# Attention's pieces on SyncE's row: two rates for keys and queries, and the weight fetch ahead of the pieces

## The chip, the cores and the metric

The kernel runs on one core of a Trainium2 chip. The core has a matrix engine (TensorE, PE in the rows, with its weight loads shown apart as PEld), a vector engine (VectorE, DVE), a scalar engine (ScalarE, ACT), GpSimd (POOL) and SyncE (SP), which here issues the transfers between the chip's main memory (DRAM) and the core's own memory (SBUF). Every engine works its instructions off in one fixed row and stands still where the next of them waits for another engine or for a transfer. TensorE writes its products into PSUM, a small memory of eight banks.

The metric is the time of one execution on the device, in microseconds (us); the median of several runs counts.

## What is computed

Windowed attention with a few memory keys, then two products with a maximum between, then two products with a piecewise function between. All of it is float32.

```python
# attention: B, H, S, D = 4, 8, 768, 64; 8 memory keys
for c in range(24):                                   # chunks of 32 queries
    q_c   = q[:, :, 32*c : 32*c + 32]
    k_ctx = k[:, :, max(0, 32*c - 16) : min(S, 32*c + 32 + 8)]     # v_ctx alike
    s = concat([mem_k, k_ctx]) . q_c / 8
    out[:, :, 32*c : 32*c + 32] = softmax(s) @ concat([mem_v, v_ctx])
x = out as (3072 tokens, 512)
# first MLP, 512 -> 768 -> 512
h = max(x @ w1, x @ w2, x @ w3);  x = h @ w_out
# second MLP, 512 -> 2048 -> 512
h = x @ w_in
g = h where h >= 1, 0 where h <= -1, (h + 1)**2 / 4 between
out = g @ w_out2
```

## The kernel before

A float32 product is made of three faster ones: each operand is split into a high and a low part, and `mm3` (L499 to L501) adds high x high, high x low and low x high into the same bank. These three lines are most of TensorE's work.

The tokens go through the first MLP in six blocks of 512. Attention goes in 24 units of 128 tokens, four to a block. The loop over `order` (its body begins where `last_block = done = 0` is set) is one slot for each product group of the first MLP: a slot runs its products (`slot_l1` or `slot_l2`), then one `att_step()`, which is a sixth of an attention unit, then copies of finished products out of PSUM, splits, and last a few transfers. `steps(u)` yields the six parts of a unit: the first has the product with the values of the unit before (`st_o`, L426) and the scores (`st_s`, L378); the second asks for the next values (`load_v`, eight transfers at L265, always into the same buffer `vw`); the third flips keys and queries. So `part`, which is `done % 6`, counts slots within a unit, shifted by one: it is taken after `done` was raised.

**Keys and queries.** They come as many small transfers, called pieces here, because the transposes that "flip" them on VectorE want them laid out in a certain way: 32 rows of 32 elements for each chunk. `load_ks` puts 20 pieces for three units of keys into the list `queue` (16 of 32x12x32 elements and 4 narrow ones for the edge), ahead of whatever queries are still in it; they go into the buffer `kq`. `load_qs` appends 16 pieces for two units of queries (32x8x32 elements), which go in turn into two tiles `qs` and into `kT2`. `feed` takes pieces from the front of the list and issues them on SP, in each slot as many as a table says. `flip_k` and `flip_q` first issue whatever the list still holds (L352, L360), and then transpose what has come (L355, L356, L363).

**Weights of the second MLP.** Beside this, the loop prepares combined weights for the second MLP. `round_step` does one step of that for each slot, by the part: "p" (part 1) and "b" (part 5) combine on VectorE, "out a" (part 3) stores the weights combined last to DRAM (five stores, L948 to L952, for the first weights; two, L954 and L955, for the later ones) and has ScalarE take the absolute value of the next ones (`abs_w`, L134), and "in in" (part 4) fetches two more weights (`fetch_w`, L119 or L121) into a staging tile `st`, of which there are two. The fetch of part 4 writes the tile that the stores of part 3 have just read.

**SP's row.** Every transfer of the kernel is issued by SP, in the order in which the program is written (`manual_schedule`): pieces, values, stores, fetches, and outputs of finished blocks (`yd`, L1107). A transfer that must wait, for a buffer or for another transfer, holds all that stand behind it.

The lines of a slot around the change, and the table of parts:

```python
    BY_PART = "", "p", "", "out a", "in in", "b"
    ...
                part = 5 if s == 3 else done % 6
                feed((5, 6, 4, 6, 5, 1)[part])
                round_step(BY_PART[part].split() + (["a"] if s == 1 else []))
```

Of the kernel before, what the change touches and what calls it, by code (L numbers as in the profile page):

```python
# [64 lines left out]
def attention_then_two_mlps(ctx, tc, q, k, v, mem_k, mem_v, w1, w2, w3, w_mid, w_in, w_out, out):  # L65
# [218 lines left out]
    def fill_mk(u):  # L284
        b = u // UPB
        if held["kw"] != b:
            copy("km", u)(
                out=kw[:, :, :, 0:NM],
                in_=memkT[:, :, b:b + 1, :].to_broadcast([P, HP, NC, NM]))
            held["kw"] = b  # L290
# [18 lines left out]
    NB3 = 3 * NC  # L309
    ks = kq[:, 0:HP * (NB3 + 1) * CH].rearrange("p (h c d) -> p h c d", h=HP, d=CH)  # L310
    qs = {}
    queue = []

    def quadrants(src, h, t0, rows, n):
        for e in range(2):
            for x in range(2):
                yield (2 * e + x) * 32, src[2 * h + e, t0:t0 + n * CH, 32 * x:32 * x + 32].rearrange(
                    "(c t) d -> t c d", t=rows)

    def load_ks(g):  # L320
        b, s0 = divmod(3 * g, UPB)
        t0 = s0 * P - LEFT
        c0 = 1 if t0 < 0 else 0
        later = queue[:]
        del queue[:]
        for h in range(HP):
            for r, a in quadrants(k[b], h, t0 + c0 * CH, CH, NB3):
                queue.append(partial(nc.sync.dma_start, out=ks[r:r + CH, h, c0:c0 + NB3, :], in_=a))
        r0, c, t = (LEFT, 0, 0) if c0 else (0, NB3, S - LEFT)
        for e in range(2):  # L330
            for x in range(2):
                r = (2 * e + x) * 32 + r0
                queue.append(partial(
                    nc.sync.dma_start, out=ks[r:r + LEFT, :, c, :],
                    in_=k[b].rearrange("(h e) t d -> e t h d", e=2)[e, t:t + LEFT, :, 32 * x:32 * x + 32]))
        queue.extend(later)
# [11 lines left out]
                queue.append(partial(nc.sync.dma_start, out=qs[g][h // 2][r:r + CH, h % 2], in_=a))  # L348

    def flip_k(u):  # L350
        while queue:
            queue.pop(0)()  # L352
        c = u % 3 * NC
        fill_mk(u)
        nc.vector.transpose(out=kw[:, :, :, NM:NM + CH], in_=ks[:, :, c:c + NC, :])  # L355
        nc.vector.transpose(out=kw[:, :, :, NM + CH:NM + 2 * CH], in_=ks[:, :, c + 1:c + 1 + NC, :])  # L356

    def flip_q(u):
        while queue:
            queue.pop(0)()  # L360
        c = u % 2 * NC
        for i, t in enumerate(qs[u // 2]):
            nc.vector.transpose(out=qTb[u % 2][:, 2 * i:2 * i + 2], in_=t[:, :, c:c + NC, :])  # L363
# [129 lines left out]
    def att_step():  # L493
        for s in todo.pop() if todo else ():
            run(*s)
# [40 lines left out]
    def l1_split(j, f, m):  # L536
        if m == 2:
            split(("A", j, f), cur.pop(("t", j, f)), f"a{j}_{f}")
# [81 lines left out]
    def split_c():  # L620
        s = put[0]
        if s >= limit[0]:
            return
        n, k = divmod(s, 7)
        t = raw[2 * n + (k >= PARTS)][:, PRODUCTS[k][0] % PARTS]
        cs[s] = next_half()
        c = cs[s].rearrange("p (u f) -> p u f", u=2)
        nc.scalar.copy(out=c[:, 0], in_=t)  # L628
        nc.gpsimd.tensor_tensor(out=c[:, 1], in0=t, in1=c[:, 0].bitcast(F32), op=ALU.subtract)  # L629
        put[0] += 1  # L630
        if k in (PARTS - 1, 6) and loaded[0] < total // 7 * 2:
            del raw[2 * n + (k >= PARTS)]
            load_c(loaded[0])
            loaded[0] += 1
# [300 lines left out]

    fetched, rounded, kept = [2 * Q1 + 4], [Q1], []

    def feed(room):
        while queue and room > 0:
            queue.pop(0)()  # L940
            room -= 1

    def round_step(acts):
        if "out" in acts and kept:
            q, c, d = kept.pop(0)
# [28 lines left out]
    BY_PART = "", "p", "", "out a", "in in", "b"  # L974

    with tc.manual_schedule(engines={ENG.PE, ENG.DVE, ENG.Activation, ENG.Pool, ENG.SP}):
# [67 lines left out]
        def w_tile(name):  # L1044
            return wpool.tile([P, 2, TB], F32, tag="w", name=name)

        last_block = done = 0
        for s, (f, *a) in enumerate(order):
            j = a[0]
            if f is not slot_l2 and j == NB - 1 and last_block == 0:  # L1050
                while todo:
                    att_step()
                att.close()
                rp = ctx.enter_context(tc.tile_pool(name="rp", bufs=1, side="right"))
                last_block = s
                hb.append(rp.tile([P, TB], F32R, tag="hb0", name="hb0"))
                hb.extend(mx.tile([P, TB], F32R, tag="y", name=f"hb{i}", bufs=2) for i in (1, 2))
                fb.extend(rp.tile([P, TB], F32, tag=f"f{i}", name=f"f{i}") for i in range(6))
                hq["h12", 2] = [rp.tile([P, TB], F32, tag=f"h{i}", name=f"h12_{i}") for i in (4, 5)]
                for g in (0, 1):  # L1060
                    hq["h22", g] = rp.tile([P, 2, TB], F32, tag=f"a{g}", name=f"h22_{g}")
            made, out_now = unsplit[:], stores[:]
            del stores[:]
            f(*a)
            if last_block:
                made = unsplit[:]
            else:

                for _ in range(2 if s in (2, 3) else 1):
                    att_step()  # L1070
                    done += 1
                for _ in range(2):
                    if evictions:
                        evictions.pop(0)()

            for x in made:
                l1_split(*x)
                unsplit.remove(x)
            if last_block:
                t = s - last_block  # L1080
                round_step(["out"])
                if t == 1:
                    for g in (2, 3):
                        hq["h22", g] = w_tile(f"h22_{g}")
                for name in LAST_BLOCK.get(t, "").split():
                    if name == "c":
                        split_c()
                    elif name == "raw":
                        load_c(loaded[0])
                        loaded[0] += 1  # L1090
                    elif name == "r":
                        load_d(t - 4)
                    elif name == "d":
                        i = len(resident)
                        split_d(i)
                        if i + 2 < len(RESIDENT):
                            load_d(i + 2)
                    elif name == "E":
                        hq["h21", 0] = w_tile("h21_0")
                    else:  # L1100
                        prep(0, name)
            else:
                part = 5 if s == 3 else done % 6
                feed((5, 6, 4, 6, 5, 1)[part])
                round_step(BY_PART[part].split() + (["a"] if s == 1 else []))
                for store in out_now:
                    store()  # L1107
        for x in unsplit:
# [81 lines left out]
```

## Time and profile before

| | |
|---|---|
| median of 3 runs | 969.0 us (968.9 to 969.28) |
| the profiled execution | 968.48 us, of which its instructions span 966.7 us |
| mean granted clock of TensorE | 0.987 of full speed |
| TensorE busy | 945.5 us, 98% of the span |
| VectorE, ScalarE, GpSimd busy | 705.2, 542.2, 339.5 us |
| transfers | 142.81 MB, 148 GB/s on average, queue of the kernel's own transfers 51.2% of 16 DMA engines' time |

The loop with attention in it runs to about 440 us of the span; after it come the last block of the first MLP and the second MLP, which hold none of the pieces. In the rows below, a start is in us from the start of the span. "x8" is a number of instructions that are shown as one row, with the time from the first's start to the last's end. "SPq" is SP's row of issues: the time there is that of issuing, not of moving the data. "[3.32 <-ACT t L532]" is idle time ahead of an instruction and what ended it.

### The profile page before, as it was taken

The numbers are of one execution on the slowest core, as the hardware profiler recorded it, in microseconds if no ns is written. First come the engines' busy times: TensorE is split into PE (matmuls) and PEld (weight loads), VectorE is DVE, ScalarE is ACT, GpSimd is POOL, SyncE is SP. The second block draws the span as 40 slices with busy tenths as digits, with TensorE's granted clock in tenths as the row PEclk, the third lists the DMA queues.
The fourth block names the chain that finished last, engine by engine and source line by source line (L and its number), as shares of the span: only waits on it lengthen the run. The fifth ranks groups of instructions, "written<-read, shape, count | busy, mean of one in ns | idle before, by whom it ended". The sixth has DMA issues, their size and how long they took to land.

```text
span 966.7 us, 18906 instructions
## 1 busy us (share of the span) xinstructions
PE 945.5 (98%) x7090; PEld 777.7 (80%) x7090; DVE 705.2 (73%) x1001; ACT 542.2 (56%) x972; POOL 339.5 (35%) x330
## 2 busy tenths in 40 slices
PE   6799999999989999999999999999999999999998
PEld 5688887888868888888888888888888888888886
DVE  3999947687766777762436777997777998777855
ACT  5766644342324223322438777676777776777763
POOL 0000003222321010110656555555566555665542
PEclk8799999999999999999999999999999999999999
DMA  7886646657667576524314237525235644322723
GB/s 183 221 221 194 167 132 162 162 148 219 186 194 193 141 183 205 190 93 155 115 38 154 81 94 277 159 61 120 76 98 181 229 120 89 98 87 87 262 66 66
DMA packets 242779, 142.81 MB, mean 148 GB/s; under 512 B 174464, under 2 KB 210176, under 8 KB 242688
## 3 DMA queue, kind: packets, MB, share of 16 engines
q1 hardware_dynamic: 242688, 141.60, 51.2%
q8 instruction: 56, 0.92, 0.4%
q14 instruction: 35, 0.29, 0.1%
HBM read 109.71 MB, written 31.46 MB: 146 GB/s over the span
## 4 chain that ended last, share of the span: by engine, by line
PE 93%; DVE 2%; DMA 2%; SPq 1%; ACT 1%; issue 1%; POOL 0%; POOLq 0%; DVEq 0%; ACTq 0%
PE psums L499 29%; PE psums L501 28%; PE psums L500 28%; PE psums L426 2%; PE psums L378 2%; PE psums L410 1%; PE psums L273 1%; DMA kq<-in_k_dram 1%; DMA kq<-in_q_dram 0%; PE psums L304 0%; PE psums L1011 0%; DMA vw<-in_v_dram 0%; SPq L360 0%; SPq L265 0%; SPq L940 0%
## 5 line engine op out<-in xcount | busy, mean ns | idle before, releaser
L518 POOL TENSOR_TENSOR hl_a<-t,hh_a 128x512 fp32r<-128x512 f32 x30 | 41.0, 1366 | 394.3 <-ACT hh_a L516 375.8
L499 PE MATMUL psums<-xh,hi 128*128 128x512 f32 x432 | 173.4, 401 | 3.3 <-ACT t L532 3.3
L501 PE MATMUL psums<-xh,lo 128*128 128x512 f32 x432 | 169.4, 392 | 0.0
L500 PE MATMUL psums<-xl,hi 128*128 128x512 f32 x432 | 169.2, 392 | 0.2 <-DVE xl L440 0.2
L809 POOL TENSOR_TENSOR hb<-h,hb 128x512 fp32r<-128x512 f32 x72 | 99.5, 1382 | 92.5 <-PE psums L501 59.5
L801 ACT CAST hb<-h 128x512 fp32r<-128x512 f32 x144 | 88.8, 622 | 48.1 <-PE psums L500 46.5
L499 PEld LDWEIGHTS psums<-xh,hi 128*128 128x128 f32 x432 | 81.8, 189 | 20.3 <-ACT t L532 3.7
L501 PEld LDWEIGHTS psums<-xh,lo 128*128 128x128 f32 x432 | 81.7, 189 | 17.8
L534 DVE TENSOR_TENSOR t<-psums,t 128x512 f32<-128x512 f32 x72 | 49.4, 686 | 63.9 <-PE psums L501 63.9
L629 POOL TENSOR_TENSOR hb<-ra,hb 128x256 fp32r<-128x256 f32 x96 | 75.4, 797 | 58.7 <-ACT hb L628 56.3
L500 PEld LDWEIGHTS psums<-xl,hi 128*128 128x128 f32 x432 | 81.8, 189 | 16.5 <-DVE xl L440 0.7
L693 ACT ACTIVATE psums<-h 128x512 f32<-128x512 f32 x96 | 57.9, 603 | 59.9 <-DVE h L779 24.2
L501 PE MATMUL psums<-t,hb 128*128 128x512 f32 x192 | 74.8, 390 | 0.0
L500 PE MATMUL psums<-t,hb 128*128 128x512 f32 x192 | 74.7, 389 | 0.0
L499 PE MATMUL psums<-t,hb 128*128 128x512 f32 x192 | 74.7, 389 | 0.0
L629 POOL TENSOR_TENSOR hb<-rb,hb 128x256 fp32r<-128x256 f32 x72 | 55.7, 780 | 39.2 <-ACT hb L628 39.2
L807 DVE TENSOR_TENSOR hb<-psums,hb 128x512 fp32r<-128x512 f32 x66 | 44.9, 680 | 24.8 <-PE psums L501 21.3
L694 ACT ACTIVATE psums<-psums 128x512 f32<-128x512 f32 x96 | 55.9, 582 | 3.1
L499 PE MATMUL psums<-hh_a,hi 128*128 128x512 f32 x144 | 57.5, 399 | 0.0
L832 DVE TENSOR_TENSOR h<-h,h 128x1024 f32<-128x1024 f32 (+1 forms) x42 | 56.5, 1368 | 0.0
L500 PE MATMUL psums<-hl_a,hi 128*128 128x512 f32 x144 | 56.2, 390 | 0.0
L501 PE MATMUL psums<-hh_a,lo 128*128 128x512 f32 x144 | 56.2, 390 | 0.0
(145 smaller groups left out, 2244.9 us busy)
## 6 DMA issues: line engine op xcount, KB each, us to landing
t<-td SPq DMA_DIRECT2D x15, 1024.0 KB
ra<-cd SPq DMA_DIRECT2D x24, 512.0 KB
st<-in_moe_w_out_dram SPq DMA_DIRECT2D x22, 512.0 KB
st<-in_moe_w_dram SPq DMA_DIRECT2D x18, 512.0 KB
vw<-in_v_dram SPq DMA_DIRECT2D x152, 56.0 KB
st<-in_moe_w_in_dram SPq DMA_DIRECT2D x16, 512.0 KB
h<-yd SPq DMA_DIRECT2D x12, 512.0 KB
rb<-cd SPq DMA_DIRECT2D x24, 256.0 KB
```

What stands on the lines that cost most here:

```text
L499: nc.tensor.matmul(out, whi, xhi, start=first, stop=False)
L500: nc.tensor.matmul(out, whi, xlo, start=False, stop=False)
L501: nc.tensor.matmul(out, wlo, xhi, start=False, stop=last)
L518: e.tensor_tensor(out=lo, in0=h, in1=hi.bitcast(F32), op=ALU.subtract)
L534: nc.vector.tensor_tensor(out=cur["t", j, f], in0=s, in1=cur["t", j, f], op=ALU.max)
L629: nc.gpsimd.tensor_tensor(out=c[:, 1], in0=t, in1=c[:, 0].bitcast(F32), op=ALU.subtract)
L693: nc.scalar.activation(out=a, in_=x, func=AF.Relu, bias=0.5, scale=0.5)
L694: nc.scalar.activation(out=a, in_=a, func=AF.Square)
L801: nc.scalar.copy(out=hi, in_=x)
L807: nc.vector.tensor_tensor(out=lo, in0=y, in1=hi.bitcast(F32), op=ALU.subtract)
L809: nc.gpsimd.tensor_tensor(out=lo, in0=x, in1=hi.bitcast(F32), op=ALU.subtract)
L832: nc.vector.tensor_tensor(out=x, in0=y, in1=z, op=op)
```

## The change

No transfer and no instruction is added or taken away; the places of transfers on SP's row are changed.

- `send(n)` takes the place of `feed(room)` and of the loops in `flip_k` and `flip_q`. It also counts down `urgent`, the number of key pieces that are still in the list (they stand at its front).
- While there are key pieces in the list, the table is the old one: 5, 6, 4, 6, 5, 1 pieces for the six parts. While there are only queries, it is 3, 4, 2, 4, 3, 0. The table is chosen by what is in the list before a slot's pieces are sent.
- In part 4 `round_step`, with its fetch of two weights, comes ahead of the slot's pieces. In the other parts it stays behind them.

```diff
--- before.py
+++ after.py
@@ -309,13 +309,18 @@
     NB3 = 3 * NC
     ks = kq[:, 0:HP * (NB3 + 1) * CH].rearrange("p (h c d) -> p h c d", h=HP, d=CH)
     qs = {}
-    queue = []
+    queue, urgent = [], [0]
 
     def quadrants(src, h, t0, rows, n):
         for e in range(2):
             for x in range(2):
                 yield (2 * e + x) * 32, src[2 * h + e, t0:t0 + n * CH, 32 * x:32 * x + 32].rearrange(
                     "(c t) d -> t c d", t=rows)
+
+    def send(n):
+        for _ in range(min(n, len(queue))):
+            queue.pop(0)()
+            urgent[0] = max(urgent[0] - 1, 0)
 
     def load_ks(g):
         b, s0 = divmod(3 * g, UPB)
@@ -325,11 +330,13 @@
         del queue[:]
         for h in range(HP):
             for r, a in quadrants(k[b], h, t0 + c0 * CH, CH, NB3):
+                urgent[0] += 1
                 queue.append(partial(nc.sync.dma_start, out=ks[r:r + CH, h, c0:c0 + NB3, :], in_=a))
         r0, c, t = (LEFT, 0, 0) if c0 else (0, NB3, S - LEFT)
         for e in range(2):
             for x in range(2):
                 r = (2 * e + x) * 32 + r0
+                urgent[0] += 1
                 queue.append(partial(
                     nc.sync.dma_start, out=ks[r:r + LEFT, :, c, :],
                     in_=k[b].rearrange("(h e) t d -> e t h d", e=2)[e, t:t + LEFT, :, 32 * x:32 * x + 32]))
@@ -348,16 +355,14 @@
                 queue.append(partial(nc.sync.dma_start, out=qs[g][h // 2][r:r + CH, h % 2], in_=a))
 
     def flip_k(u):
-        while queue:
-            queue.pop(0)()
+        send(len(queue))
         c = u % 3 * NC
         fill_mk(u)
         nc.vector.transpose(out=kw[:, :, :, NM:NM + CH], in_=ks[:, :, c:c + NC, :])
         nc.vector.transpose(out=kw[:, :, :, NM + CH:NM + 2 * CH], in_=ks[:, :, c + 1:c + 1 + NC, :])
 
     def flip_q(u):
-        while queue:
-            queue.pop(0)()
+        send(len(queue))
         c = u % 2 * NC
         for i, t in enumerate(qs[u // 2]):
             nc.vector.transpose(out=qTb[u % 2][:, 2 * i:2 * i + 2], in_=t[:, :, c:c + NC, :])
@@ -935,11 +940,6 @@
 
     fetched, rounded, kept = [2 * Q1 + 4], [Q1], []
 
-    def feed(room):
-        while queue and room > 0:
-            queue.pop(0)()
-            room -= 1
-
     def round_step(acts):
         if "out" in acts and kept:
             q, c, d = kept.pop(0)
@@ -1101,8 +1101,12 @@
                         prep(0, name)
             else:
                 part = 5 if s == 3 else done % 6
-                feed((5, 6, 4, 6, 5, 1)[part])
-                round_step(BY_PART[part].split() + (["a"] if s == 1 else []))
+                acts = BY_PART[part].split() + (["a"] if s == 1 else [])
+                if part == 4:
+                    round_step(acts)
+                send(((5, 6, 4, 6, 5, 1) if urgent[0] else (3, 4, 2, 4, 3, 0))[part])
+                if part != 4:
+                    round_step(acts)
                 for store in out_now:
                     store()
         for x in unsplit:
```

How it moves transfers on SP's row, at three places. The names: `qs_0` and `qs_1` are the two tiles of a group of queries, `kT_82` is the buffer `kT2` of the next group, `kq` is the buffer of the keys, `vw` that of the values, `st` a staging tile, and L948 to L952 are the five stores; in the changed kernel all pieces are issued at L322, in `send`.

The first place is the first group of queries that is loaded by `load_qs`, with the stores and the fetch that fall into it. Before:

```order
L940 DMA qs_0_1849<-in_q_dram 32x8x32 x8
L940 DMA qs_1_1850<-in_q_dram 32x8x32 x2
L948 DMA td<-st_1603 128x4x256
L949 DMA td<-st_1603 128x2x256
L950 DMA td<-c_1670 128x2x256
L951 DMA rd<-c_1670 128x2x256
L952 DMA rd<-st_1603 128x256
L940 DMA qs_1_1850<-in_q_dram 32x8x32 x5
L119 DMA st_1913<-in_moe_w_out_dram 128x1024 x2
L940 DMA qs_1_1850<-in_q_dram 32x8x32
L265 DMA vw<-in_v_dram 56x4x64 x8
L940 DMA kq<-in_k_dram 32x12x32 x10
```

and now:

```order
L322 DMA qs_0_1849<-in_q_dram 32x8x32 x6
L948 DMA td<-st_1603 128x4x256
L949 DMA td<-st_1603 128x2x256
L950 DMA td<-c_1670 128x2x256
L951 DMA rd<-c_1670 128x2x256
L952 DMA rd<-st_1603 128x256
L119 DMA st_1904<-in_moe_w_out_dram 128x1024 x2
L322 DMA qs_0_1849<-in_q_dram 32x8x32 x2
L322 DMA qs_1_1850<-in_q_dram 32x8x32 x4
L265 DMA vw<-in_v_dram 56x4x64 x8
L322 DMA qs_1_1850<-in_q_dram 32x8x32 x4
L322 DMA kq<-in_k_dram 32x12x32 x10
```

The fetch has gone from behind five pieces to right behind the last store, six pieces go ahead of the stores instead of ten, and four pieces have come to stand behind the eight loads of values.

The second place is the group of keys after it. Before:

```order
L940 DMA kq<-in_k_dram 32x12x32 x10
L948 DMA td<-st_2354 128x4x256
L949 DMA td<-st_2354 128x2x256
L950 DMA td<-c_2547 128x2x256
L951 DMA rd<-c_2547 128x2x256
L952 DMA rd<-st_2354 128x256
L940 DMA kq<-in_k_dram 32x12x32 x5
L119 DMA st_2805<-in_moe_w_out_dram 128x1024 x2
L940 DMA kq<-in_k_dram 32x12x32
L940 DMA kq<-in_k_dram 16x4x32 x4
L265 DMA vw<-in_v_dram 56x4x64 x8
```

and now:

```order
L322 DMA kq<-in_k_dram 32x12x32 x10
L948 DMA td<-st_2354 128x4x256
L949 DMA td<-st_2354 128x2x256
L950 DMA td<-c_2543 128x2x256
L951 DMA rd<-c_2543 128x2x256
L952 DMA rd<-st_2354 128x256
L119 DMA st_2800<-in_moe_w_out_dram 128x1024 x2
L322 DMA kq<-in_k_dram 32x12x32 x6
L322 DMA kq<-in_k_dram 16x4x32 x4
L265 DMA vw<-in_v_dram 56x4x64 x8
```

The number of pieces ahead of the values is the same; the fetch goes ahead of the keys that came before it.

The third place follows at once: queries, the next stores, and the fetch of the unit after. Before:

```order
L940 DMA kT_82<-in_q_dram 32x8x32 x10
L948 DMA td<-st_2571 128x4x256
L949 DMA td<-st_2571 128x2x256
L950 DMA td<-c_2780 128x2x256
L951 DMA rd<-c_2780 128x2x256
L952 DMA rd<-st_2571 128x256
L352 DMA kT_82<-in_q_dram 32x8x32 x6
L119 DMA st_3023<-in_moe_w_out_dram 128x1024 x2
L265 DMA vw<-in_v_dram 56x4x64 x8
```

and now:

```order
L322 DMA kT_82<-in_q_dram 32x8x32 x6
L948 DMA td<-st_2562 128x4x256
L949 DMA td<-st_2562 128x2x256
L950 DMA td<-c_2780 128x2x256
L951 DMA rd<-c_2780 128x2x256
L952 DMA rd<-st_2562 128x256
L322 DMA kT_82<-in_q_dram 32x8x32 x10
L119 DMA st_3023<-in_moe_w_out_dram 128x1024 x2
L265 DMA vw<-in_v_dram 56x4x64 x8
```

Six queries instead of ten go ahead of the stores, the ten others behind them; here they are sent by `flip_k`, which comes ahead of the slot's `round_step`, and so the fetch stands behind ten pieces instead of six.

## Rows read from the trace of the kernel before

**Rows 1.** The page's first part: busy time of each engine, share, instructions.

```profile
PE 945.5 (98%) x7090; PEld 777.7 (80%) x7090; DVE 705.2 (73%) x1001; ACT 542.2 (56%) x972; POOL 339.5 (35%) x330
```

**Rows 2.** TensorE's waits, 140 to 440 us: us in total, times, longest.

```profile
PE psums L499 <- ACT t L532: 3.3, 1, 3.3
```

**Rows 3.** Timeline of TensorE, 237 to 282 us: start, time, instruction, wait before.

```profile
237.66 1.14 PE L426 MATMUL psums<-aT,vw 64*64 64x32 f32 x64
...
256.55 1.14 PE L426 MATMUL psums<-aT,vw 64*64 64x32 f32 x64
...
276.12 0.61 PE L499 MATMUL psums<-xh,hi 128*128 128x512 f32 x1 [3.32 <-ACT t L532]
...
280.65 1.14 PE L426 MATMUL psums<-aT,vw 64*64 64x32 f32 x64
```

**Rows 4.** Stretches: length, busy PE, PEld, DVE, ACT, POOL; granted clock, DMA share, GB/s.

```profile
160.00:255.00 95.00, 94.77 (x1024) 77.74 (x1023) 68.91 (x107) 36.11 (x56) 23.25 (x17) 1.00 0.68 180
255.00:282.00 27.00, 23.68 (x309) 18.91 (x308) 20.36 (x32) 7.18 (x11) 5.11 (x4) 0.94 0.70 198
```

**Rows 5.** Timeline of ScalarE, the abs of two units.

```profile
251.44 1.12 ACT L134 ACTIVATE c<-st 128x1024 f32<-128x1024 f32 x1 [2.39 <-DMA st<-in_moe_w_out_dram]
...
273.45 1.13 ACT L134 ACTIVATE c<-st 128x1024 f32<-128x1024 f32 x1 [5.00 <-DMA st<-in_moe_w_out_dram]
```

**Rows 6.** Timeline of SP's issues, 161 to 269 us, pieces, fetches and values.

```profile
161.98 4.34 SPq L265 DMA_DIRECT2D vw<-in_v_dram  x8
...
176.21 2.79 SPq L940 DMA_DIRECT2D kq<-in_k_dram  x5
179.10 0.89 SPq L119 DMA_DIRECT2D st<-in_moe_w_out_dram  x2
...
220.03 3.50 SPq L940 DMA_DIRECT2D qs<-in_q_dram  x5
223.91 0.83 SPq L119 DMA_DIRECT2D st<-in_moe_w_out_dram  x2
...
243.31 2.52 SPq L940 DMA_DIRECT2D kq<-in_k_dram  x5
246.15 0.83 SPq L119 DMA_DIRECT2D st<-in_moe_w_out_dram  x2
...
249.47 4.98 SPq L265 DMA_DIRECT2D vw<-in_v_dram  x8
...
268.09 0.87 SPq L119 DMA_DIRECT2D st<-in_moe_w_out_dram  x2
```

**Rows 7.** Waits of SP's row, 150 to 270 us: us in total, times, longest.

```profile
SPq L265 <- DMA st<-in_moe_w_out_dram: 4.9, 4, 1.9
SPq L119 <- DMA rd<-st: 4.4, 3, 3.8
SPq L265 <- PE psums L426: 2.8, 1, 2.8
```

**Rows 8.** Timeline of SP's issues where a fetch follows the stores at once.

```profile
198.30 0.69 SPq L952 DMA_DIRECT2D rd<-st  x1
202.92 1.58 SPq L119 DMA_DIRECT2D st<-in_moe_w_out_dram  x2
...
276.70 0.67 SPq L952 DMA_DIRECT2D rd<-st  x1
279.55 0.92 SPq L121 DMA_DIRECT2D st<-in_moe_w_in_dram  x2
```

**Rows 9.** The chain of waits in order of time, at 194 us: one piece's transfer.

```profile
194.41 1.84 DMA kT<-in_q_dram
```

**Rows 10.** Waits of SP's row, 280 to 300 us.

```profile
SPq L940 <- DVE qTb L363: 4.0, 1, 4.0
```

**Rows 11.** Timeline of SP's issues, 298 to 304 us.

```profile
298.89 3.79 SPq L940 DMA_DIRECT2D kq<-in_k_dram  x5
302.78 0.97 SPq L121 DMA_DIRECT2D st<-in_moe_w_in_dram  x2
```

## The prediction, made before the changed kernel ran

> **What bounds the kernel now.** Read the page first: TensorE is busy in 945.5 of 966.7 us [rows 1], so the change can only give back idle time of TensorE or add some. Ask then where TensorE waits in the stretch that the change touches (140 to 440 us, the first layer's loop): it is one wait of 3.3 us, for ScalarE's copy of a product (L532) [rows 2]. Two of TensorE's steps measure what that wait costs. The attention part of a unit (L426) recurs after 18.89 us (237.66 to 256.55) and then after 24.10 us (256.55 to 280.65) [rows 3]: 5.2 us lost, 3.3 of them the wait and 1.9 after it, when the matmuls run slower. The granted clock of 255 to 282 us is 0.94, against 1.00 before [rows 4], so part of this stretch stood at the lower level, 1.2 GHz. The wait is not ScalarE's own: its abs of the second MLP's weights (L134), which stands ahead of that copy, sat idle for 5.00 us until a weight fetch had landed, at 273.45, and a unit earlier for 2.39 us, which TensorE did not feel [rows 5].
>
> Why is the fetch late? SP issues every transfer of this kernel in one row, and it is behind. The fetch of 268.09 [rows 6] belongs, in the program, to part 4 of the unit whose L426 started at 237.66; a part is a sixth of 18.89 us, so TensorE was there at about 250. A piece costs SP 0.50 us (five in 2.52 at 243.31), eight loads of values 4.98 at 249.47 [rows 6]. From 161.98 us on SP has work without a break; the last time it waited for TensorE was just before, 2.8 us, for the values' buffer [rows 7]. So from 162 to 280 us SP sets when data comes, and whatever adds to SP's time in this stretch arrives at TensorE once the slack is gone.
>
> **The change part by part.** It adds and removes no instruction of any engine; every transfer is the same. It moves transfers on SP's row alone, so the question is what each one now waits for.
>
> *1. The fetch in front of the pieces of part 4.* Before, the five stores of the combined weights (L948 to L952) are followed by five pieces and then the fetch. Now the fetch follows the last store at once. But it writes the staging buffer that these stores read: it must wait until they have landed. Where nothing stands between in the trace of before, SP idles: L952 ends at 198.99 and the fetch goes at 202.92, 3.9 us; it ends at 277.37 and the fetch goes at 279.55, 2.2 us [rows 8]. From 150 to 270 us this wait (rd<-st) came to 4.4 us in three places, one of them 3.8 [rows 7]. Where five pieces stand between, they use that time: from 176.21 to 179.00, fetch at 179.10; from 220.03 to 223.53, fetch at 223.91; from 243.31 to 245.83, fetch at 246.15 [rows 6]. Now this cover is gone: SP stands, and the five pieces are still to be issued afterwards. Each such place costs the landing time less what was waited already. At the first, the fetch did not wait, so the stores had landed by 2.9 us after L952; the shortest case seen is 2.2: I take 2.5. At the second the fetch went 3.9 us after L952 ended (219.98) with 0.4 of it idle: 3.5. At the third 2.8 less 0.3: 2.5. Together 8.5 us; with 2.2 us at each place it would be 5.9, with 3.9 at the two later ones 10.0. At the fetch of 202.92 nothing changes: it stood alone before too.
>
> Queued behind the waiting fetch are all of the keys' pieces, the next values and the next stores; waiting for these are TensorE (L426 reads the values), VectorE (the flips of keys) and ScalarE (the abs).
>
> The Trainium skill, "DMA: Bandwidth & Descriptors", section "Anatomy of one DMA", gives 2.0 us plus the bytes at 436 GB/s for a DMA of the GpSimd path, most of the 2.0 being the receipt of the write. By it, as an estimate, the five stores (1.44 MB) would be down 5.3 us after the first issue, so 1.8 us after L952's issue ended; the rows show 2.2 to 3.9. By the page the three places would cost 4.5 us instead of 8.5, and the end would be near 978. I go by the rows.
>
> *2. Queries at 3, 4, 2, 4, 3, 0.* Before, the first group's 16 pieces are all out before the values of 161.98, in time that SP would have idled; now four of them come behind these values (first pair of rows in the section on the change): 4 x 0.50 = 2.0 us that SP does not get back, as it has no idle time after. For the later groups the split moves pieces across values or fetch, but ahead of the values of 249.47 stand the same transfers as before. Cost 2.0 us; at most that, and 0 if SP finds time I don't see.
>
> *3. The flush.* At the fetch of 268.09 the change does the opposite of its words: the slower rate leaves ten queries instead of six, the flush of flip_k sends them, and the fetch goes behind them. Ahead of it stand the same transfers as before in all, so it cannot go earlier; its lateness is SP's.
>
> *4. The sum up to 281 us.* SP is late by 2.0 + 8.5 = 10.5 us at the values of 249.47. These have hardly slack: the last of the eight is issued at 254.1, a piece lands some 1.84 us later [rows 9], 255.9, and L426 starts at 256.55; it reads the last piece in the course of 1.14 us. Slack 0.6 to 1.7, say 1.0. TensorE is held 9.5 us, and the clock costs 1.9 us again after so long a pause. The abs at that place is late as well, behind the same row, and hides under this hold. The fetch that caused the old wait then lands at 273.45 + 10.5 = 283.95; ScalarE is ready at 268.45 + 9.5 + 1.9 = 279.85 and waits 4.1 instead of 5.0, so the old loss of 5.2 shrinks by 0.9 and stays otherwise. Net 9.5 + 1.9 - 0.9 = 10.5 us, which is SP's lateness, as it should be for a row that sets the pace. With the bounds of step 1 it is about 7 to 12.
>
> *5. After 281 us.* SP waits for TensorE's and VectorE's buffers again (the keys of the next group start after 4.0 us of waiting for VectorE's flip of the old queries [rows 10]) and begins afresh; the time lost stays lost. Then the same pattern again: the fetch of 302.78 followed five keys (298.89 to 302.68 [rows 11]) without waiting, and two more fetches of this stretch have pieces in front of them. Three stalls of 2.2 to 3.9, less 1.0 that was waited anyway, and four queries moved past values: 6 to 11 us of SP's time, against a slack that I can't price well, as ScalarE's waits here did not reach TensorE. Between 0 and 8 us; I take 3, nearer the lower end, since the keys start this stretch on time.
>
> Sum 10.5 + 3.0 = 13.5 us on the profiled execution of 968.5 (span 966.7 and 1.8 around it): 982.0; the median of the runs, 969.0, lies 0.5 above the profiled one. Forecast **982 us**, own range 976 to 990.
>
> **The rivals.**
> *A, faster: the fetches become quick.* SP also waits for fetches: the values behind one wait 4.9 us in four places for it to land [rows 7]. If a fetch that leaves when the stores are done, with fewer pieces on the DMA engines, landed so much earlier that these four waits went, and if the stores' landing were mostly over when L952 has been issued, SP would gain 4.9 less 2.0, 2.9 us; the fetch of 268.09 would go that much earlier, 2.9 of the 3.3 us of wait and the 1.9 of clock would go: 4.8 us, 964. It decides where the stalls of step 1 add up to less than 2.9 us. For it: the weights are what ScalarE waits for. Against it: 3.9 and 2.2 us in the two places where nothing stood between [rows 8], and the fetches of 179.10 and 246.15 met no store traffic either. Chance 0.11.
>
> *B, no change: the lateness is swallowed.* If the values of 249.47 had 5 us more slack than I think, or the stalls fell where SP would stand anyway, the old wait would stay and nothing be added: 967 to 971. Against it is the abs, which waited already 2.39 and 5.00 us for SP's row. Chance 0.10.
>
> *C, slower still: the holds add up.* If every hold costs the clock's 1.9 us anew, three or four times, and the second stretch comes at its 8 us: 13.5 + 5 + 4 to 6, so 991 to 994. It decides if TensorE stands in more than two places. Chance 0.09.
>
> **How the numbers follow.** The forecast has 0.70. A run of this kernel can tell about 0.2% (1.9 us) from no change. Slower by more than that: forecast and C, 0.79; within: B, 0.10; faster: A, 0.11. The range 968 to 990 takes in most of B and leaves out A and C, 0.20.
>
> **What the next profile would show.** Right: SP waits for the stores' landing (rd) before nearly each fetch, 2 to 4 us each and some 15 us more in all than now; TensorE's waits at L426 or L378 near 256 us for values or keys, 5 to 10 us; the wait at L499 after it still there; the distance from L426 to L426 far above 18.9 us in two units; a dip of the clock in both. Wrong: fetches that leave within 1 us of the last store (step 1), values issued at 249 to 252 as before (the sum), or TensorE's waits after 140 us under 4 us in all with a faster end (A). If only the part up to 281 is as told, step 5 was mis-sized.

## The result, and the profile after

The changed kernel takes **978.9 us** (median of 4 runs, 977.84 to 981.48), the kernel before 968.95 (4 runs, 967.47 to 969.28): a ratio of 1.0109, with a 95% interval of 1.0087 to 1.0132. That is about 10 us slower. 982 was forecast, and 978.9 lies within the forecast's own range of 976 to 990. The profiled execution took 979.18 us, its span is 977.4 us: 10.7 more than before.

The page's first part answers to [rows 1]: TensorE is busy 5.3 us more, though it does the same work. So part of the loss is counted as busy time: matmuls at a lower clock, and, as the rows further down show, matmuls that take their data piece by piece as it lands.

```profile
PE 950.8 (97%) x7090; PEld 780.5 (80%) x7090; DVE 703.9 (72%) x1001; ACT 541.3 (55%) x972; POOL 339.6 (35%) x330
```

TensorE's waits of the changed kernel from 140 to 460 us that are over 1 us (us in all, times, longest) answer to [rows 2]. Shorter ones are left out there and here: 0.8 and 0.2 us before, 0.8, 0.2 and 0.2 now. Lines in the middle of the file are 5 higher now: L431 was L426, L504 was L499, L537 was L532.

```profile
PE psums L431 <- DMA vw<-in_v_dram: 4.9, 11, 2.3
PE psums L504 <- ACT t L537: 1.6, 1, 1.6
```

The wait that was there is shorter, 1.6 us instead of 3.3, and a new one has come: for the values. TensorE's timeline shows it, beside [rows 3]:

```profile
236.61 0.85 PE L431 MATMUL psums<-aT,vw 64*64 64x32 f32 x24
...
238.10 0.78 PE L431 MATMUL psums<-aT,vw 64*64 64x32 f32 x38 [0.16 <-DMA vw<-in_v_dram]
...
259.05 0.70 PE L431 MATMUL psums<-aT,vw 64*64 64x32 f32 x8 [2.34 <-DMA vw<-in_v_dram]
...
261.70 2.12 PE L431 MATMUL psums<-aT,vw 64*64 64x32 f32 x46 [0.28 <-DMA vw<-in_v_dram]
...
282.49 0.50 PE L504 MATMUL psums<-xh,hi 128*128 128x512 f32 x1 [1.58 <-ACT t L537]
...
285.45 1.14 PE L431 MATMUL psums<-aT,vw 64*64 64x32 f32 x64
```

L431 starts 22.44 us after the unit before (236.61 to 259.05) where 18.88 is the rule, and works until 263.8 piece by piece as the values land, 4.8 us instead of 1.14. It did so in the unit before as well, in a smaller way: 2.3 us, from 236.61 to 238.88. The next distance is 26.39 (259.05 to 285.45); before it was 24.11. The stretches of both kernels that hold the dip (length, busy time of the five engines, granted clock, DMA share, GB/s) answer to [rows 4]: 0.89 here, 0.94 before.

```profile
160.00:255.00 95.00, 94.42 (x1019) 77.41 (x1019) 65.91 (x102) 33.76 (x54) 23.24 (x17) 1.00 0.61 164
255.00:285.45 30.45, 25.37 (x213) 19.70 (x211) 19.26 (x30) 9.24 (x13) 5.12 (x4) 0.89 0.70 186
```

And SP's issues, beside [rows 6] and [rows 8]: the last store, the fetch behind it, the ten keys, and the values.

```profile
176.75 0.68 SPq L952 DMA_DIRECT2D rd<-st  x1
179.64 0.83 SPq L119 DMA_DIRECT2D st<-in_moe_w_out_dram  x2
180.52 6.87 SPq L322 DMA_DIRECT2D kq<-in_k_dram  x10
...
219.57 0.67 SPq L952 DMA_DIRECT2D rd<-st  x1
224.21 0.83 SPq L119 DMA_DIRECT2D st<-in_moe_w_out_dram  x2
...
247.46 0.71 SPq L952 DMA_DIRECT2D rd<-st  x1
250.32 0.83 SPq L119 DMA_DIRECT2D st<-in_moe_w_out_dram  x2
251.20 5.77 SPq L322 DMA_DIRECT2D kq<-in_k_dram  x10
257.07 3.87 SPq L265 DMA_DIRECT2D vw<-in_v_dram  x8
```

From the end of the last store to the fetch, SP stands 2.2, 4.0 and 2.2 us (177.43 to 179.64, 220.24 to 224.21, 248.17 to 250.32), where five pieces stood before. The values that went at 249.47 go at 257.07. SP's waits from 150 to 270 us say the same in sum, beside [rows 7]:

```profile
SPq L119 <- DMA rd<-st: 12.4, 5, 3.8
SPq L322 <- DMA st<-in_moe_w_out_dram: 1.5, 2, 1.2
SPq L265 <- DMA st<-in_moe_w_out_dram: 0.8, 1, 0.8
```

Fetches wait 12.4 us for stores instead of 4.4; values wait 0.8 us for fetches instead of 4.9, and keys, which never did, 1.5.

One table puts the loss together. It lists, for each kernel, the distances from unit to unit (starts of L426 or L431 in TensorE's timeline, from unit 10, at 237.66 in [rows 3], on) that are off 18.88 us, and their excess in sum. The units are counted so that 11 starts at 256.55 and 12 at 280.65 before. All other distances are 18.87 to 18.96.

| kernel | distances off 18.88 us, ending at unit | excess |
|---|---|---|
| before | 12: 24.11 | 5.2 |
| changed | 11: 22.44, 12: 26.39, 15: 20.09, 16: 22.16, 18: 20.29 | 17.0 |
| fetch_first | 11: 22.39, 12: 26.55, 16: 20.29, 18: 22.73 | 16.4 |
| fetch_first_half | 11: 21.15, 12: 27.17 | 10.6 |
| rates_only | 11: 19.04, 12: 28.39, 18: 20.01 | 10.8 |
| rates_later | 12: 24.26, 18: 19.86 | 6.4 |
| no_store_wait | 12: 23.48 | 4.6 |
| stores_earlier | 12: 27.30 | 8.4 |
| keys_flush | 10: 19.46, 11: 23.41, 12: 23.93, 14: 19.61, 15: 24.81, 18: 19.25 | 17.2 |
| stores_keys | 11: 19.71, 12: 24.11 | 6.1 |
| stores_oldrate | 12: 23.64 | 4.8 |
| stores_keys_oldrate | 12: 19.67, 16: 20.63 | 2.5 |
| pool_fetch | 12: 22.25, 16: 20.59 | 5.1 |
| stores_keys_pool | 12: 21.52, 16: 19.77 | 3.5 |

Before and changed differ by 11.8 in this column; the changed execution reached the loop 1.1 us sooner, which its code has no part in (the first instruction that it moves is later), and 10.7 remain, the difference of the spans. The table is of one execution each and does not hold that start, so times below are by ratios of medians and the table says where they come from.

### The profile page after: what moved, and what is told of

It reads as the page before. It is cut to its first block, busy times and chain, and to the rows that moved or that the text cites. A ratio compares the mean times of both kernels' runs of the same rounds, so it can differ in the third digit from the quotient of the medians.

```text
span 977.4 us, 18916 instructions
## 1 busy us (share of the span) xinstructions
PE 950.8 (97%) x7090; PEld 780.5 (80%) x7090; DVE 703.9 (72%) x1001; ACT 541.3 (55%) x972; POOL 339.6 (35%) x330
## 4 chain that ended last, share of the span: by engine, by line
PE 85%; SPq 5%; DMA 4%; DVE 4%; ACT 2%; issue 1%; DVEq 0%; ACTq 0%
PE psums L504 27%; PE psums L506 26%; PE psums L505 26%; PE psums L431 2%; SPq L322 2%; PE psums L383 2%; SPq L265 1%; DMA vw<-in_v_dram 1%; PE psums L415 1%; DMA kq<-in_q_dram 1%; DMA rd<-st 1%; PE psums L304 0%; ACT c L134 0%; PE psums L273 0%; DVE c L150 0%
## 5 line engine op out<-in xcount | busy, mean ns | idle before, releaser
L504 PE MATMUL psums<-xh,hi 128*128 128x512 f32 x432 | 173.7, 402 | 1.8 <-ACT t L537 1.6
L504 PEld LDWEIGHTS psums<-xh,hi 128*128 128x128 f32 x432 | 81.9, 190 | 19.2 <-ACT t L537 2.0
L504 PE MATMUL psums<-t,hb 128*128 128x512 f32 x192 | 74.7, 389 | 0.0
L142 DVE TENSOR_SCALAR c<-c 128x1024 f32<-128x1024 f32 x28 | 20.6, 735 | 56.8 <-ACT c L134 43.0
L504 PE MATMUL psums<-hh_a,hi 128*128 128x512 f32 x144 | 57.5, 399 | 0.0
```

Source lines behind the costliest of these rows:

```text
L504: nc.tensor.matmul(out, whi, xhi, start=first, stop=False)
```

## Experiments

Each ratio below is against the kernel before as it ran on the same chip at that time (medians of 967.9 to 969.3 us), so times of different runs are best compared by their ratios.

Theory W: a fetch right behind the stores of its own staging tile stands on SP's row until they have landed, and all that is queued behind is late. Its rivals: R, the lower rate of the queries does it; D, the fetch's megabyte, now ahead of the pieces, makes these late. The diffs are against the changed kernel where nothing else is said; `slow` stands there for `((5, 6, 4, 6, 5, 1) if urgent[0] else (3, 4, 2, 4, 3, 0))[part]`, and `old` for `(5, 6, 4, 6, 5, 1)[part]`.

**One part of the change at a time.** fetch_first has only the new place of the fetch:

```diff
-                send(slow)
+                send(old)
```

> The changed kernel with the old table (5, 6, 4, 6, 5, 1) for all pieces: only the place of the fetch in part 4 is changed. Theory W (the fetch now stands on SP's row until the stores of the same staging tile have landed, and all behind it is late): 976 to 981 us, nearly the whole loss, and SP's waits of fetches for stores come to 30 us or more between 140 and 460 us, against 21 before. Rival R (it is the lower rate of the queries, which puts them behind values and fetches): 967 to 971 us. Rival D (the fetch does not wait long, but its megabyte goes ahead of the pieces on the DMA engines and makes these land late): 976 to 981 us too.

Measured: 982.8 us, 1.0131 (1.0102 to 1.0159) of the kernel before, somewhat above the 976 to 981 that W and D expected. The place of the fetch alone brings the whole loss, and the waits of fetches for stores from 140 to 460 us come to 36 us in this run, as W has it. rates_only has only the rates:

```diff
-                if part == 4:
+                if False:
                     round_step(acts)
                 send(slow)
-                if part != 4:
+                if True:
                     round_step(acts)
```

> The changed kernel with the fetch of part 4 behind the pieces again: only the two rates are changed. Theory W: 968 to 971 us, no more than the 2.0 us that the four queries behind the values cost. Rival R: 975 to 980 us. Rival D: 968 to 971 us.

Measured: 971.2 us, 1.0020 (1.0004 to 1.0037). About 2 us; R falls as the main cause. The profiled execution shows more than that, 5.6 us over the kernel before in the table, 4.3 of them at unit 12 and 1.1 at unit 18.

**The wait taken away, the order kept.** In no_store_wait the stores read something else, a resident weight tile, so the combined weights of the loop are not stored:

```diff
+    first_w = []
...
         split2[q] = hi, lo
+        first_w.append(hi)
...
             q, c, d = kept.pop(0)
+            if not last_block:
+                d = first_w[0].bitcast(F32).rearrange("p i (a f) -> p (i a) f", a=2)
...
-                nc.sync.dma_start(out=td[0:4, f, :, 0, :].rearrange("m p c -> p m c"), in_=d[:, 3:7])
+                nc.sync.dma_start(out=td[0:4, f, :, 0, :].rearrange("m p c -> p m c"), in_=d[:, -4:])
...
-                nc.sync.dma_start(out=cd[q - Q2][:, 4:7], in_=d)
+                nc.sync.dma_start(out=cd[q - Q2][:, 4:7], in_=d[:, 0:3])
```

> The changed kernel, but until the last block of the first MLP the stores that read a staging tile read a resident weight tile of the first MLP instead, as many bytes in the same shapes to the same places; so the second MLP's weights are wrong, and the fetch has nothing to wait for on the stores' side. The order of SP's row stays. Theory W: the 12 us of these waits between 150 and 270 us are gone, the values of the unit at 257 us come in time, and the fetch after is earlier than in the kernel before: 962 to 969 us. Rival R: 976 to 980 us, since the order is the same. Rival D: 975 to 980 us, since the fetch is still ahead of the pieces, and earlier.

Measured: 969.55 us, 0.9997 (0.9983 to 1.0012): the loss is gone, with the fetch still ahead of the pieces, and no fetch waits for a store from 150 to 270 us. W holds, though the time is half a us above its range, and D falls as a cause of the 10 us. But D has a grain of truth, which may be why this run does not beat the kernel before. SP's timeline of this run, at the place of the second pair of order rows:

```profile
242.02 0.78 SPq L956 DMA_DIRECT2D rd<-hi  x1
242.90 1.32 SPq L120 DMA_DIRECT2D st<-in_moe_w_out_dram  x2
244.27 6.98 SPq L324 DMA_DIRECT2D kq<-in_k_dram  x10
251.34 3.60 SPq L267 DMA_DIRECT2D vw<-in_v_dram  x8
```

The fetch goes 0.1 us after the last store, but ten keys behind it take SP 6.98 us, where five ahead of it and five behind took 2.52 [rows 6] and 2.35 in the kernel before:

```profile
247.02 2.35 SPq L940 DMA_DIRECT2D kq<-in_k_dram  x5
```

Not all ten are slower: one of them, the sixth, takes 2.25 us, and the others 0.3 to 0.6. And TensorE's wait for ScalarE at unit 12 is still 2.8 us:

```profile
PE psums L506 <- ACT t L539: 2.8, 1, 2.8
```

**The wait covered.** stores_earlier puts the stores into part 2, so that the pieces of part 3 stand between them and the fetch:

```diff
-    BY_PART = "", "p", "", "out a", "in in", "b"
+    BY_PART = "", "p", "out", "a", "in in", "b"
```

> The changed kernel with the stores of part 3 in part 2, so that the pieces of part 3 stand between them and the fetch; the fetch is still ahead of part 4's pieces. Theory W: 963 to 969 us, the fetch waits under 1 us where pieces stand between and 2 to 4 us in the units without pieces. Rival R and rival D: 975 to 980 us.

Measured: 970.8 us, 1.0018 (1.0006 to 1.0030). W's direction, 0.9% better than the changed kernel, but 2 us above what was expected: TensorE's wait for ScalarE at unit 12 is 4.1 us in this run. So there is a second wait beside the fetch's own.

**The second wait.** Theory F: the fetch ahead of unit 12 is late because `flip_k` sends all queries that are in the list ahead of it. keys_flush sends the keys alone:

```diff
     def flip_k(u):
-        send(len(queue))
+        send(urgent[0])
```

> The changed kernel, where the flip of keys sends only the key pieces that are left, not the queries behind them: at the fetch after the unit of 257 us six queries instead of sixteen stand ahead of it. It asks what the other wait is, TensorE's for ScalarE behind that fetch, which is there in all kernels so far. Theory F (that fetch is late because the flush puts ten queries, 5.9 us of SP's time, ahead of it): the fetch goes some 3.8 us earlier than in the changed kernel (5.9 less a stores' landing of 2.2), TensorE's wait of 1.6 us and its part of the slow clock go, 974 to 977 us. Rival G (it is late because SP is late anyway, whatever the order): 977 to 981 us.

Measured: 981.4 us, 1.0124 (1.0090 to 1.0159), above the 974 to 977 of theory F. TensorE's wait of 1.6 us for ScalarE is gone as F says, but the total is not better: the table has 24.81 us at unit 15, where the changed kernel has 20.09. What is gained at one place is lost at another; by what path is not shown. With the stores a part earlier, the same edit (stores_keys):

> The stores a part earlier, as in the run before, and the flip of keys sends only keys. Theory F: the fetch has 6 queries ahead of it instead of 16, goes some 5 us earlier than in the kernel with earlier stores alone, TensorE's wait of 4.1 us for ScalarE goes, with its slow clock; no wait of a fetch for stores over 1 us in the units with pieces: 962 to 966 us, faster than both kernels. Rival G: 968 to 972 us.

Measured: 969.04 us, 1.0000 (0.9982 to 1.0018): within no change, at the place where rival G put it, though the wait for ScalarE is gone here too. With the old table as well (stores_keys_oldrate):

> The same with the old table for all pieces. If the lower rate costs only the four queries behind the values (2 us of SP's time), that is saved, but ten queries stand ahead of the fetch in question instead of six, 2 us more: theory F 962 to 967 us, no clear difference to the run with the lower rate. Rival R (the lower rate is what costs): 2 to 4 us less than with the lower rate.

Measured: **961.3 us, 0.9916 (0.9887 to 0.9944): faster than both kernels**, by the lower rate's going, which I had expected to change little. Whether the new place of the fetch adds to this gain was not tried: no run has the earlier stores and the flush of keys alone with the fetch behind the pieces. TensorE's waits of this run from 140 to 440 us, all that there are:

```profile
PE psums L415 <- DVE p L409: 0.8, 1, 0.8
PE psums L504 <- ACT t L537: 0.5, 1, 0.5
PE psums L431 <- DMA vw<-in_v_dram: 0.3, 1, 0.3
PE psums L505 <- DVE xl L445: 0.2, 1, 0.2
PE psums L504 <- DVE t L539: 0.2, 1, 0.2
```

And SP's timeline at the fetch in question: six queries between the last store and the fetch, and 0.1 us of standing.

```profile
259.32 1.38 SPq L952 DMA_DIRECT2D rd<-st  x1
260.75 4.22 SPq L322 DMA_DIRECT2D kT<-in_q_dram  x6
265.07 0.88 SPq L119 DMA_DIRECT2D st<-in_moe_w_out_dram  x2
265.99 2.90 SPq L322 DMA_DIRECT2D kT<-in_q_dram  x6
```

The profiled execution took 965.7 us. The six fall into two sets: four from 960.8 to 961.4 us with a mean granted clock of 0.994 to 0.996, and two, the profiled one among them, of 965.7 and 966.4 us with 0.991 and 0.987. So the median is that of executions of which no trace here shows the waits. To part the edits, stores_oldrate has the earlier stores, the new place of the fetch and the old table, and sends all pieces at the flip:

> Stores a part earlier, fetch ahead of the pieces, old table, and the flip of keys sends all pieces again. It parts the two edits of the fastest run so far (961.3 us). If the earlier stores with the old table bring the gain: 961 to 964 us. If the flush of keys alone is needed as well: 966 to 970 us, with twelve pieces instead of six after the stores and ahead of the fetch of the unit after 257 us, 3 us of SP's time, and TensorE's wait for ScalarE there of 3 us.

Measured: 968.7 us, 1.0013 (0.9992 to 1.0034). So the keys' flush is needed as well. Nor does the old table bring anything clear by itself, as stores_earlier, with the lower rate, has 1.0018: it takes the two together. And F is right here: twelve queries stand after the stores and ahead of the fetch, and TensorE waits 2.9 us for ScalarE instead of 0.5.

```profile
259.25 6.89 SPq L322 DMA_DIRECT2D kT<-in_q_dram  x12
266.19 0.92 SPq L119 DMA_DIRECT2D st<-in_moe_w_out_dram  x2
```

**The two stretches.** fetch_first_half has the fetch ahead of the pieces only up to 281 us:

```diff
-                if part == 4:
+                first = part == 4 and fetched[0] < len(conv) and conv[fetched[0]][0] == "d"
+                if first:
                     round_step(acts)
-                send(slow)
-                if part != 4:
+                send(old)
+                if not first:
                     round_step(acts)
```

> The fetch ahead of the pieces, with the old table, for the first half of the weights only (the fetches at L119, up to 270 us); the later ones (L121) stay behind the pieces. It parts the loss up to 281 us from the loss after it. If SP begins afresh after 281 us, as the prediction has it, the later loss of some 5 us in the run with all fetches first is a loss of its own and goes: 974 to 977 us. If SP's lateness is carried from the first stretch into the second: 978 to 983 us, as with all fetches first.

Measured: 974.0 us, 1.0057 (1.0034 to 1.0080), 5.5 us over the kernel before. After unit 12 every distance is 18.88 in the table: the later loss is one of its own, as the prediction has it. rates_later parts the lower rate:

```diff
-                if part == 4:
+                if False:
                     round_step(acts)
-                send(slow)
+                send(((5, 6, 4, 6, 5, 1) if urgent[0] or len(qs) < 2 else (3, 4, 2, 4, 3, 0))[part])
-                if part != 4:
+                if True:
                     round_step(acts)
```

> The two rates alone, with the first group of queries sent at the old rate. If the four queries of that group behind the values are the whole cost of the lower rate, as the prediction has it: 968 to 970 us. If the later groups cost too (four queries behind the values there, ten instead of six in the flush): 970 to 973 us, as with the rates alone.

Measured: 969.0 us, 1.0022 (0.9999 to 1.0046): the first expectation's time, but its ratio is that of the rates alone (1.0020), and its interval covers both expectations. In the table unit 12 is back at 24.26, which is the first expectation's, but from one execution; it stays open.

**SP relieved.** pool_fetch is the kernel before with the loop's fetches issued by GpSimd:

```diff
+    issue = [nc.sync]
...
+        dma = issue[0].dma_start
...
-            nc.sync.dma_start(out=st.rearrange("p f t -> p (f t)"), in_=src[j * P:(j + 1) * P, :])
+            dma(out=st.rearrange("p f t -> p (f t)"), in_=src[j * P:(j + 1) * P, :])
...
         last_block = done = 0
+        issue[0] = nc.gpsimd
```

> The kernel before, with the fetches of the loop issued by GpSimd instead of SP, so that nothing of SP's row waits for the stores on their account, and a fetch waits for nothing but its staging tile. Theory W with F: SP's row loses 0.9 us of issuing and 1 to 4 us of waiting for each fetch, the fetches leave as soon as the stores have landed, TensorE's wait of 3.3 us goes: 962 to 966 us. Rival G or a GpSimd that is itself late (its own work stands ahead of the fetch in its row): 968 us or more.

Measured: 967.0 us, 0.9976 (0.9959 to 0.9992): faster, but by 2 us only. TensorE's wait for ScalarE is gone; it waits for GpSimd in its place. GpSimd's timeline, then TensorE's:

```profile
264.51 1.09 POOL L122 DMA_DIRECT2D st<-in_moe_w_out_dram  x2 [14.50 <-DMA rd<-st]
265.62 1.28 POOL L521 TENSOR_TENSOR hl_a<-t,hh_a 128x512 fp32r<-128x512 f32 x1
```

```profile
266.95 0.50 PE L503 MATMUL psums<-hl_a,hi 128*128 128x512 f32 x1 [3.07 <-POOL hl_a L521]
```

The fetch stands 14.5 us at the head of GpSimd's row, until the stores have landed, and the subtraction that TensorE needs stands behind it. The same with the edits of the fastest run (stores_keys_pool):

> The fastest run so far with the fetches of the loop issued by GpSimd. If SP's row still holds TensorE anywhere, the 0.9 us of each fetch and the pieces' waits for it are gained: 958 to 961 us. If TensorE's waits in this stretch, 2.0 us in all in that run, are what is left: 960 to 962 us. If a fetch that waits in GpSimd's row holds the subtraction behind it, for which TensorE waited 3.1 us with GpSimd's fetches alone: 963 us or more.

Measured: 965.2 us, 0.9973 (0.9953 to 0.9993): its third expectation, and TensorE waits 2.3 us for the same subtraction. Whichever engine issues the fetch, its row is held by the stores.

## Why the prediction was right, and where it was not

*What bounds the kernel.* Right: SP's row sets the pace of the loop from 162 to 280 us. no_store_wait takes a wait off that row and leaves its order, and the ratio falls from 1.0109 to 0.9997, some 11 us.

*Step 1, the fetch and the stores.* Right, with its price. 8.5 us were forecast for the three places; the rows give 2.2, 4.0 and 2.2, less the 0.10, 0.38 and 0.32 us that were waited there before: 7.5. (The upper bound of 10.0 takes 2.9 at the first place too; with the 2.5 used there it is 9.6.) The estimate by the Trainium skill's page "DMA: Bandwidth & Descriptors", section "Anatomy of one DMA", was 1.8 us from the last store's issue to its landing; 2.2 to 4.0 were measured, and the rows of the kernel before were the better price. That the end of 978 by that estimate is near the measured one is no proof of it, since other terms were off.

*Step 2, the four queries.* 2.0 forecast; the rates alone cost 2 us by the medians. In this kernel the bound "at most that" held: fetch_first, without the lower rate, is no faster than the changed kernel. It does not hold as a price of the lower rate by itself: with the stores earlier and the flush of keys alone, the same lower rate costs 0.84% or some 8 us (stores_keys against stores_keys_oldrate, on the same chip), 3.6 of them in the table's distances.

*Step 3, the flush.* The flush was priced at nothing, since ahead of the fetch stand the same transfers in all. It held in the changed kernel, where letting the queries wait gained nothing (keys_flush). It doesn't hold as a price of the flush by itself: with the stores' wait covered it is worth 0.97% (stores_oldrate against stores_keys_oldrate; these two did not run on the same chip).

*Step 4, the sum up to 281 us.* This is the term that was mis-sized: 10.5 us forecast, 5.9 measured (the distances at units 11 and 12, 48.83 instead of 42.99). The 10.5 were 9.5 of hold and 1.9 of clock, less 0.9 that the old loss of 5.2 was to shrink; measured are 7.2 of hold and 2.3 of clock, less 3.6.

The hold first. SP was late by 8.7 at the values, not 10.5: 257.07 less 249.47 and the 1.1 us by which the execution was ahead. Two terms were missing. The values' waits for fetches fell by 4.1 us, which is what rival A had spoken of; and the ten keys behind a fetch took longer (6.87 and 5.77 us, against 5.14 and 4.87 for five and five), 2.6 in all. Nearly all of that is one key each time, the sixth:

```profile
183.12 2.35 SPq L322 DMA_DIRECT2D kq<-in_k_dram  x1
...
253.72 1.34 SPq L322 DMA_DIRECT2D kq<-in_k_dram  x1
```

With the 7.5 and 2.0 us of steps 1 and 2 these terms make 8.0; the rest is small differences. One of them is the fetch of 202.92, at which nothing was to change: the wait there fell from 3.9 us to 2.8. Of the 8.7 TensorE lost 7.2 at L431: 1.1 while it took the values at 236.61, 2.3 of waiting ahead of 259.05, and 3.6 while it took the values there. So the slack was 1.5. (As waits the rows list 3.7 us at L431 up to 285 us, where the signs had 5 to 10; the rest is counted as busy.)

The old loss next. It was forecast to stay at 4.3 and came to 1.6, the wait alone. From L431's start TensorE came to that wait 5.6 us later than before, the fetch went only 3.9 later, and so 1.6 us of the 3.3 were left. And no slow matmuls followed this shorter wait. The clock fell once, at L431's second hold and behind it, and not in both units as the signs had it; the first unit was at 1.00. The unit, the slow stretch in the next and the matmuls behind the last wait (length, busy time, granted clock):

```profile
236.61:259.05 22.44, 19.76 (x205) 16.03 (x205) 10.84 (x17) 6.10 (x9) 4.25 (x3) 1.00 0.67 166
263.75:268.44 4.69, 4.69 (x76) 3.75 (x73) 3.09 (x6) 1.99 (x4) 0.14 (x1) 0.50 0.67 206
282.49:285.45 2.96, 2.96 (x13) 2.17 (x13) 2.93 (x4) 0.00 (x0) 0.00 (x0) 1.00 0.96 324
```

0.50 is the lower level of 1.2 GHz. This one dip cost what remains, 48.83 less 37.76 less 7.2 and 1.6: 2.3 us.

*Step 5, after 281 us.* 3.0 forecast, within 0 to 8; 5.9 measured (1.2, 3.3 and 1.4 at units 15, 16 and 18). It begins afresh, as told (fetch_first_half). The 6 to 11 us of SP's time that the step gives hold the stalls alone; with the 2.0 of its four queries it would be 7.6 to 12.7. I had taken the low end because the waits looked hidden, and TensorE's waits from 285 to 450 us are indeed 1.4 us in all:

```profile
PE psums L431 <- DMA vw<-in_v_dram: 1.2, 5, 0.3
PE psums L504 <- DVE t L539: 0.2, 1, 0.2
```

Most of the loss is counted as busy. At the starts of these three distances L431 takes the values as they land, 2.4, 2.5 and 2.6 us instead of 1.14 (323.21 to 325.57, 343.29 to 345.78, 384.33 to 386.89): 4.0 of the 5.9 us. The clock adds to it at one of the three. The first and the last of these units, and two parts of the one between (length, busy time, granted clock):

```profile
323.21:343.29 20.08, 19.57 (x205) 16.00 (x204) 9.67 (x18) 3.92 (x6) 1.28 (x1) 1.00 0.54 146
345.71:350.30 4.59, 4.35 (x79) 3.45 (x74) 4.45 (x7) 1.59 (x3) 1.55 (x1) 0.63 0.66 222
350.30:365.45 15.15, 15.15 (x69) 12.25 (x67) 12.33 (x21) 4.30 (x6) 1.30 (x1) 1.00 0.60 135
384.33:404.63 20.30, 19.86 (x206) 16.10 (x205) 16.41 (x27) 5.63 (x9) 2.57 (x2) 1.00 0.72 232
```

From 345.71 to 350.30 the granted clock is 0.63, that is, in part at the lower level of 1.2 GHz; this stretch and the wait of 0.2 us in it are the other 1.9 us.

So 10.5 and 3.0 were forecast, 5.9 and 5.9 were measured: the sum was nearer than its parts, and that it came within some 3 us is in part luck, one part being too high and the other too low. *Rivals:* A's waits of the values did go, 4.1 us, but against 7.5 of stalls they did not decide; B and C did not come.

## What to carry to other kernels

Where one engine issues all transfers, a transfer that must wait for another is priced by what used to stand between the two: work in that gap is free, and a transfer moved out of it is paid twice, by the standing and by the work that comes after. So look, ahead of such a move, for what the moved transfer waits for; and move the store that it waits for too, if it can go earlier. A flush that sends more than the next step reads is the same fault in another place.

## What the runs showed of the hardware

- Five stores of 1.44 MB had landed 2.1 to 4.0 us after the last one's issue ended, by the fetches that waited for them at five places of the changed kernel (the first at 154.16 us), and the spread is between places of one kernel.
- Of ten keys right behind a fetch of two times 512 KB, up to 281 us, the sixth took SP 2.35 and 1.34 us (changed kernel) and 1.71 and 2.25 us (no_store_wait, once with the eighth at 1.78), where the others took 0.3 to 0.6; the ten took 5.8 to 7.6 us. The profile puts 1.5 us in two places of the changed kernel down to a wait for the fetch, which these keys neither read nor write. In the kernel before and the changed one, ten keys with no fetch right ahead of them took 4.9 to 6.3 us, so the total alone does not tell the two apart.
- Matmuls that take their data as it lands count as busy: at three places L431 took 2.4 to 2.6 us instead of 1.14, with 0.3 to 0.5 us of waiting listed. A loss can stand in a busy row.
- A wait of 3.3 us (kernel before) was followed by matmuls at the lower clock, one of 1.6 us (changed kernel, 282.49) was not; 0.3 and 0.2 us, one soon after the other beside a drawn-out L431 (344.67 and 346.81), were followed by a granted clock of 0.63 over 4.6 us.
